# A planner that serves its transfer queue first come, first served: one line of the scheduling rule and a table of offsets

## The chip, the cores and the metric

The kernel runs on one core of a Trainium2 chip. The metric is device time in microseconds for one execution. The five engines are called PE (TensorE), DVE (VectorE), ACT (ScalarE), POOL (GpSimd) and SP (SyncE, which here issues nearly all transfers).

## The reference

Eight batches, eight heads, 576 positions, head size 64. A causal attention with a decay runs first; its output, joined over the heads into a 512-wide row, goes through a small gated block. Cut to what is computed:

```python
scores = 1/sqrt(D) * q @ k.T                          # per batch and head, 576 x 576
cum    = cumsum(log(clip(f, 1e-4, 1)))
scores = where(causal, -1e9, scores + cum[:, None] - cum[None, :])
attn   = exp(scores - max) ; attn /= sum + 1e-9
x      = attn @ v                                     # joined: 8 x 576 x 512
gate   = sigmoid(sum_k conv_w[k] * x shifted by k)    # 5 taps, causal, per channel
out    = (gate * (x @ w_val)) @ w_out
```

All inputs and the output are float32.

## The kernel before, in words

The work is cut into 32 **pairs** (one batch, two heads) and 8 **batches** (four pairs each). For pair i:

- `load_pair`, `load_rest`: transfers bring q, k (`qn`, `kn`, and `zn` for the last 64 rows), v (`vt`) and the decay rows (`dm`, one tile of 128x1280 per head, and `dl` for the last 64 rows). The decay table `decd` is made once at the start and lies in HBM. POOL cuts the causal edge into `dm` (L428) and `dl` (L431).
- `plan_t`: PE transposes q, k (L524) and zn (L531) into a PSUM bank; DVE or ACT copies them out, as one tile for the first four pairs (`Xf`, which lies in the second `gate` tile and is shown under that name) and as a high and a low part afterwards (`Xh`, `Xl`, L515).
- `plan_s`: PE forms the scores (L354, three groups; in the order below `gate1_114` or `Xh`/`Xl`), DVE adds the decay and takes the row extreme (L598), ACT takes the exponential and its sum (L602), DVE takes the reciprocal (L611, L612), and the normalising (`norm`, L374 on ACT, L376 on POOL or DVE) multiplies the rows `P` and `Pl`.
- `plan_pt`: PE transposes `P` (L643) and `Pl` (L661, L662); copies (L369) bring them to `pt`.
- `plan_pv`: PE multiplies `pt` with `vt` (L354, `pt,vt`), the result goes to `x`, is split into `xh` and `xl` (L712), and the five taps of the gate run on DVE (L376, L724).

Per batch, `plan_moe` adds the sigmoid on ACT (L740), the product with `w_val` (`Mv`: L354, `xh`/`xl` with `wall`), the product with the gate (L769), and the product with `w_out` (`Mo`: L354, `wall,hh` and `wall,hl`). The weights arrive in 512 KB pieces in two buffers (`wu` and the tile `ot`) and are decoded by ACT and DVE (L822 to L862).

**What sets the order.** Nothing is emitted in the order of the source. Every step above is a node of `Plan`: a class, the engines that may run it with a cost each, a priority and what it depends on. `Plan.order` then plays the program through: at each turn it looks, for each engine, at the nodes that are ready, takes those that could start within a small slack of the earliest, picks the lowest priority number among them, gives the node to that engine and moves the engine's clock. A node that several engines can run goes where this play puts it first. The result is one fixed list of instructions per engine; on the chip each engine works its list strictly in order, so a node that has to wait holds up all that stands behind it on its engine.

The priority number is the pair's place (`base`) plus an entry of the table `OFF` for the class and the stage of the program. `PEN` is a second table: a penalty on an engine for a class. `STICK` is a bonus on PE for a node of the same tiling as the one before (`mode`).

A transfer is two nodes: `hold`, the issue on SP, and `span`, the transfer itself on an engine of the play that is called `DQ` (L151 to L157). `DQ` stands for the transfer hardware: one server, with the `span` as its cost. Nothing is emitted for it; it only tells the play when the data is there. At most eight transfers are out at a time (L213 to L216).

## Time and profile before

| | us |
|---|---|
| median of 3 runs | 594.59 |
| lowest, highest of these | 593.78, 595.51 |
| the profiled execution's own time | 592.27 |
| its span, first to last instruction | 590.5 |

| engine | busy, us | share of the span |
|---|---|---|
| PE | 558.2 | 95% |
| PE weight load (PEld) | 487.5 | 83% |
| DVE | 461.3 | 78% |
| ACT | 447.9 | 76% |
| POOL | 249.9 | 42% |

Transfers move 93.43 MB in 136294 packets; the mean granted PE clock is 0.977 of full speed. How to read it: the busy shares are means over stages that differ. The profile's slices show a PE clock below 0.9 only within the first fifth of the span, and transfer hardware that is 80% busy or more in five of the first seven slices and in two later ones. So the page is read stage by stage, with the list of who waited for whom beside it.

### The profile page before, as it was taken

What the parts mean: (1) busy time and instruction counts of PE and PEld (TensorE: products, weight loads), DVE (VectorE), ACT (ScalarE), POOL (GpSimd) and SP (SyncE); (2) the same over time, 40 slices, a digit from 0 to 9 for tenths busy, and PEclk for the clock granted to TensorE, in tenths of its full rate; (3) what the DMA queues carried; (4) which work ended last, traced back from release to release, by engine and by line L of the source; (5) the groups of instructions that cost most, each with busy time, mean ns of one, the idle gap of its engine ahead of it and who ended that gap; (6) DMA issues with size and microseconds to landing.
All of it is one profiled execution on the core that took longest, in us unless ns stands there. A gap on an engine that the chain in (4) does not pass through costs nothing.

```text
span 590.5 us, 14025 instructions
## 1 busy us (share of the span) xinstructions
PE 558.2 (95%) x4693; PEld 487.5 (83%) x4693; DVE 461.3 (78%) x1238; ACT 447.9 (76%) x1217; POOL 249.9 (42%) x398
## 2 busy tenths in 40 slices
PE   8778898799889999999999999999999999999997
PEld 7546587689779998889989988899888987889885
DVE  6488979899988797788967897668879789587660
ACT  4688878999878887888887988677798876764511
POOL 3431367334322556456553746455556461210200
PEclk9779699899999999999999999999999999999999
DMA  6979898676465585757866675466776544220012
GB/s 147 266 185 266 170 240 230 166 196 168 114 183 135 143 234 158 188 136 188 188 157 167 184 189 154 117 179 152 193 201 188 159 120 123 80 83 19 37 37 89
DMA packets 136294, 93.43 MB, mean 158 GB/s; under 512 B 118474, under 2 KB 118494, under 8 KB 136222
## 3 DMA queue, kind: packets, MB, share of 16 engines
q1 hardware_dynamic: 136142, 92.52, 59.0%
q8 instruction: 37, 0.61, 0.4%
q14 instruction: 35, 0.29, 0.2%
q10 hardware_dynamic: 80, 0.02, 0.0%
HBM read 82.60 MB, written 9.91 MB: 157 GB/s over the span
## 4 chain that ended last, share of the span: by engine, by line
PE 69%; DVE 13%; DMA 8%; ACT 5%; issue 3%; SPq 1%; POOL 1%; DVEq 0%; POOLq 0%; ACTq 0%
PE banks L354 54%; PE banks L643 9%; DVE banks L598 6%; PE banks L524 3%; DMA wu<-in_moe_w_val_dram 3%; ACT P L602 3%; DMA dm<-decd 2%; DVE gate L724 2%; PE banks L661 2%; DMA qn<-in_q_dram 1%; DVE negm L598 1%; SPq L381 1%; DMA kn<-in_k_dram 1%; PE banks L531 1%; ACT P L374 1%
## 5 line engine op out<-in xcount | busy, mean ns | idle before, releaser
L602 ACT ACTIVATE P<-banks,negm 128x256 f32<-128x256 f32 (+3 forms) x256 | 131.9, 531 | 35.9 <-DVE negm L598 35.6
L369 ACT COPY pt<-banks 128x256 f32<-128x256 f32 (+2 forms) x320 | 116.9, 436 | 42.8 <-PE banks L643 36.4
L598 DVE CUSTOM_DVE_ANT_0 banks<-banks,dm 128x256 f32<-128x256 f32 (+3 forms) x256 | 120.4, 515 | 33.4 <-PE banks L354 22.2
L724 DVE SCALAR_TENSOR_TENSOR gate<-x,cw,gate 128x576 f32<-128x576 f32 x128 | 111.6, 876 | 1.7
L354 PE MATMUL banks<-xh,wall 128*128 128x288 f32 x512 | 110.2, 300 | 1.0 <-ACT ot L369 0.7
L428 POOL TENSOR_SCALAR_AFFINE_SELECT dm<-dm 128x256 f32<-128x256 f32 x126 | 57.5, 481 | 122.0 <-DMA dm<-decd 100.1
L376 POOL TENSOR_SCALAR P<-P,rz 128x128 f32<-128x128 f32 (+3 forms) x132 | 79.0, 614 | 56.5 <-DVE rz L612 32.7
L643 PE MATMUL banks<-ident,P 128*128 128x128 f32 x640 | 93.2, 283 | 9.3 <-POOL P L376 4.1
L354 PE MATMUL banks<-pt,vt 128*64 128x128 f32 (+2 forms) x1408 | 99.0, 294 | 3.2 <-DVE Xl L515 1.9
L354 PEld LDWEIGHTS banks<-pt,vt 128*64 128x64 f32 x1408 | 87.1, 139 | 16.0 <-issue 3.1
L354 PE MATMUL banks<-wall,hh 128*128 128x512 f32 x288 | 92.8, 403 | 2.8 <-ACT P L602 2.6
L643 PEld LDWEIGHTS banks<-ident,P 128*128 128x128 f32 x640 | 74.4, 144 | 20.0 <-POOL P L376 5.3
L354 PEld LDWEIGHTS banks<-xh,wall 128*128 128x128 f32 x512 | 83.8, 188 | 2.8 <-ACT ot L369 1.1
L354 PE MATMUL banks<-xl,wall 128*128 128x288 f32 x256 | 75.4, 294 | 0.0
L712 POOL TENSOR_TENSOR xl<-x,xh 128x576 fp32r<-128x576 f32 x32 | 47.1, 1475 | 46.1 <-ACT xh L369 46.1
L354 PEld LDWEIGHTS banks<-wall,hh 128*128 128x128 f32 x288 | 51.0, 188 | 13.3 <-ACT P L602 3.6
L354 PE MATMUL banks<-Xh 128*128 128x288 f32 (+2 forms) x280 | 59.1, 346 | 1.2 <-DVE Xl L515 1.0
L782 POOL TENSOR_TENSOR hl<-h,hh 128x576 fp32r<-128x576 f32 (+2 forms) x36 | 36.9, 1032 | 48.4 <-ACT hh L369 48.4
L354 PE MATMUL banks<-wall,hl 128*128 128x512 f32 x144 | 56.5, 392 | 0.0
L354 PE MATMUL banks<-Xh,Xl 128*128 128x288 f32 (+2 forms) x280 | 53.6, 315 | 0.0
L354 PE MATMUL banks<-Xl,Xh 128*128 128x288 f32 (+2 forms) x280 | 53.3, 314 | 0.0
L602 ACT ACTIVATION_READ_ACCUMULATOR P<-banks,negm 128x1 f32 x256 | 52.9, 206 | 0.0
(105 smaller groups left out, 916.7 us busy)
## 6 DMA issues: line engine op xcount, KB each, us to landing
dm<-decd SPq DMA_DIRECT2D x62, 640.0 KB, 5.4
out_dram<-ot SPq DMA_DIRECT2D x36, 256.0 KB, 2.1
dl<-decd SPq DMA_DIRECT2D x62, 144.0 KB, 3.8
qn<-in_q_dram SPq DMA_DIRECT2D x64, 128.0 KB, 3.6
kn<-in_k_dram SPq DMA_DIRECT2D x64, 128.0 KB, 5.8
vt<-in_v_dram SPq DMA_DIRECT2D x64, 128.0 KB, 2.9
zn<-in_k_dram SPq DMA_DIRECT2D x32, 32.0 KB, 3.1
vt<-in_v_dram SPq DMA_DIRECT2D x32, 32.0 KB, 3.2
```

The lines of the kernel that those rows point to most:

```text
L354: nc.tensor.matmul(out, lhsT=lhsT, rhs=rhs, start=start, stop=stop)
L369: (eng.copy if eng is nc.scalar else eng.tensor_copy)(out=out, in_=in_)
L376: eng.tensor_scalar(out=out, in0=in_, scalar1=col, scalar2=0.0, op0=ALU.mult, op1=ALU.add)
L428: nc.gpsimd.affine_select(out=t, in_=t, pattern=[[0, 2], [-1, P]], base=0, channel_multiplier=1, compare_op=ALU.is_ge, fill=-BIG)
L524: nc.tensor.transpose(out=bank(key)[:, n * P:(n + 1) * P], in_=src[:, n].rearrange("p h d -> p (h d)"), identity=ident)
L598: nc.vector.tensor_tensor_reduce(out=sl, in0=sl, in1=add[:, o:o + ext], op0=ALU.add, op1=ALU.min, scale=-0.125, scalar=3.0e38, accum_out=n ...
L602: nc.scalar.activation(out=dst[:, o:o + ext], in_=bank(key)[:, c0:c0 + ext], func=AF.Exp, bias=negm[r][:, col], scale=-1.0, accum_out=zs[r ...
L643: nc.tensor.transpose(out=bank(key)[:, c:c + P], in_=Pt[m][:, BOFF[b] + P * j:BOFF[b] + P * j + P], identity=ident)
L661: nc.tensor.transpose(out=bank(key)[:, P * j:P * j + P], in_=Pl[r][:, D + P * j:D + P * j + P], identity=ident)
L712: any_("xl", {"POOL": 1.4, "DVE": 0.67}, p, lambda eng: eng.tensor_tensor(out=xl[s], in0=xv, in1=xh[s][:, :].bitcast(F32), op=ALU.subtract ...
L724: eng.scalar_tensor_tensor(out=gt, in0=src, scalar=wt_, in1=gt, op0=ALU.mult, op1=ALU.add)
L782: eng.tensor_tensor(out=hl[jj][:, y:y + x1 - x0], in0=h32[:, x0:x1], in1=hh[jj][:, y:y + x1 - x0].bitcast(F32), op=ALU.subtract)
```

## The change

One expression of `order` is changed, together with the numbers it was tuned with. For a candidate on `DQ` the rank is no longer the node's priority but `at[n][e]`, the moment from which it could be served, so transfers are played in the order in which they became ready on the queue. `STICK` goes from 18.18 to 18.86, and nearly all entries of `OFF` and `PEN` get new values, most of them within some ten units of the old. No instruction is added or removed apart from how the play divides work: the same nodes, the same costs.

```diff
-STICK = 18.18
+STICK = 18.86
 OFF = {
-    "X": (67.59, 130.9, 49.48, 80.47, -2.55, 2.49),
+    "X": (78.48, 133.4, 48.9, 77.64, -2.11, -4.23),
-    "dec": (1.61, 60.01, -75.88, -13.59, 48.06, 86.54),
+    "dec": (-7.7, 57.47, -85.79, -27.71, 40.96, 74.69),
...
                     pen = PEN.get((nd["cls"], e), NONE)[nd["phase"]] if len(nd["engs"]) > 1 else 0.0
-                    cand.append((t + pen, nd["prio"] - (STICK if e == "PE" and nd["mode"] == mode else 0.0), n, t))
+                    cand.append((t + pen, at[n][e] if e == "DQ" else nd["prio"] - (STICK if e == "PE" and nd["mode"] == mode else 0.0), n, t))
```

Three places of the program show what this moves. In these lists `P0`, `Pl0` and so on are the buffers (with the builder's number behind the underscore), and the shape is the instruction's output.

**Place A**, POOL, pair 0 and the arrival of pair 1's first decay tile. Before:

```order
L376 TENSOR_SCALAR P0_83<-P0_83,rz0_97 128x512
L428 AFFINE_SELECT dm2_70<-dm2_70 128x2x128 x2
L376 TENSOR_SCALAR P0_83<-P0_83,rz0_97 128x256
L376 TENSOR_SCALAR P1_84<-P1_84,rz0_97 128x256
L376 TENSOR_SCALAR P0_83<-P0_83,rz0_97 128x128
L376 TENSOR_SCALAR P1_84<-P1_84,rz0_97 128x384
L376 TENSOR_SCALAR P1_84<-P1_84,rz0_97 128x128
L376 TENSOR_SCALAR Pl0_86<-Pl0_86,rz0_97 128x576
```

The same place now:

```order
L376 TENSOR_SCALAR P0_83<-P0_83,rz0_97 128x512
L376 TENSOR_SCALAR P0_83<-P0_83,rz0_97 128x256
L376 TENSOR_SCALAR P1_84<-P1_84,rz0_97 128x256
L376 TENSOR_SCALAR P0_83<-P0_83,rz0_97 128x384
L428 AFFINE_SELECT dm2_70<-dm2_70 128x2x128 x2
L376 TENSOR_SCALAR P1_84<-P1_84,rz0_97 128x128
L376 TENSOR_SCALAR Pl0_86<-Pl0_86,rz0_97 128x576
```

Three more normalisings now stand ahead of the causal cut of `dm2`, and two behind it; the 128-wide one of `P0` and the 384-wide one of `P1` went to ACT.

**Place B**, PE around the transposes of pair 4 (`qn0`, `kn0`, `zn0`), and SP where their loads are issued. PE before:

```order
L531 MATMUL banks_129<-ident_64,zn1_78 128x128 x2
L643 MATMUL banks_129<-ident_64,P2_85 128x128 x4
L643 MATMUL banks_129<-ident_64,P0_83 128x128 x4
L354 MATMUL banks_129<-gate1_114 128x384 x2
L354 MATMUL banks_129<-gate1_114 128x128 x2
L524 MATMUL banks_129<-ident_64,qn1_74 128x128 x4
L524 MATMUL banks_129<-ident_64,kn1_76 128x128 x4
L661 MATMUL banks_129<-ident_64,Pl1_87 128x128 x4
L662 MATMUL banks_129<-ident_64,Pl1_87 64x128
L524 MATMUL banks_129<-ident_64,qn0_73 128x128 x4
L524 MATMUL banks_129<-ident_64,kn0_75 128x128 x4
L531 MATMUL banks_129<-ident_64,zn0_77 128x128 x2
```

PE now:

```order
L531 MATMUL banks_129<-ident_64,zn1_78 128x128 x2
L524 MATMUL banks_129<-ident_64,qn0_73 128x128 x4
L524 MATMUL banks_129<-ident_64,kn0_75 128x128 x4
L531 MATMUL banks_129<-ident_64,zn0_77 128x128 x2
L643 MATMUL banks_129<-ident_64,P2_85 128x128 x4
L354 MATMUL banks_129<-gate1_114 128x384 x2
L354 MATMUL banks_129<-gate1_114 128x128 x2
L524 MATMUL banks_129<-ident_64,qn1_74 128x128 x4
L524 MATMUL banks_129<-ident_64,kn1_76 128x128 x4
L643 MATMUL banks_129<-ident_64,P0_83 128x128 x4
L643 MATMUL banks_129<-ident_64,P1_84 128x128 x4
L531 MATMUL banks_129<-ident_64,zn1_78 128x128 x2
```

The transposes of pair 4 went from the end of this piece to its start, a transpose of `P1` and one of pair 5's `zn1` were drawn in, and the transposes of `Pl1` with the first `pt,vt` product of pair 1 follow behind. SP before:

```order
L381 DMA zn1_78<-in_k_dram 64x2x64
L381 DMA wu_127<-in_moe_w_val_dram 128x1024
L381 DMA ot_125<-in_moe_w_val_dram 128x1024
L381 DMA qn0_73<-in_q_dram 128x4x64 x2
L381 DMA zn0_77<-in_q_dram 64x64 x2
L381 DMA kn0_75<-in_k_dram 128x4x64 x2
L381 DMA zn0_77<-in_k_dram 64x2x64
```

SP now:

```order
L381 DMA zn1_78<-in_k_dram 64x2x64
L381 DMA qn0_73<-in_q_dram 128x4x64 x2
L381 DMA zn0_77<-in_q_dram 64x64 x2
L381 DMA kn0_75<-in_k_dram 128x4x64 x2
L381 DMA zn0_77<-in_k_dram 64x2x64
L381 DMA wu_127<-in_moe_w_val_dram 128x1024
L381 DMA ot_125<-in_moe_w_val_dram 128x1024
```

The seven issues for pair 4 passed the two weight pieces.

**Place C**, PE after the first batch's sigmoid. Before:

```order
L524 MATMUL banks_129<-ident_64,kn0_75 128x128 x4
L643 MATMUL banks_129<-ident_64,P2_85 128x128 x4
L661 MATMUL banks_129<-ident_64,Pl1_87 128x128 x4
L662 MATMUL banks_129<-ident_64,Pl1_87 64x128
L354 MATMUL banks_129<-Xh1_80 128x288
L354 MATMUL banks_129<-Xh1_80,Xl1_82 128x288
L354 MATMUL banks_129<-Xl1_82,Xh1_80 128x288
```

The same place now:

```order
L524 MATMUL banks_129<-ident_64,kn0_75 128x128 x4
L643 MATMUL banks_129<-ident_64,P2_85 128x128 x4
L661 MATMUL banks_129<-ident_64,Pl1_87 128x128 x4
L662 MATMUL banks_129<-ident_64,Pl1_87 64x128
L354 MATMUL banks_129<-xh0_101,wall_126 128x288
L354 MATMUL banks_129<-xl0_107,wall_126 128x288
L354 MATMUL banks_129<-xh0_101,wall_126 128x288
```

24 `Mv` products of batch 0 now stand between the transposes of `Pl1` and the `pt,vt` products of pair 5; before, six score products and a zn transpose stood there and `Mv` began behind the `pt,vt` products. In the same way the six `Xh0` 128x288 score products of pair 4 now stand ahead of pair 2's `pt,vt` products, and before they stood behind the first half of them.

28 lines of the change are left out of this document (14 added, 14 removed), and 44 rows, old and new, of tables (OFF, PEN).

## The prediction

> **What bounds the kernel now.** The first view is the busy time of each engine in stretches of the program. A row gives the stretch, its length, the busy time of PE, PEld, DVE, ACT and POOL, the granted PE clock, the transfer hardware's busy share and its rate.
>
> ```profile
> 16.00:62.00 46.00, 35.75 (x245) 25.74 (x245) 33.15 (x90) 35.34 (x96) 17.55 (x29) 0.85 0.94 241
> 62.00:120.00 58.00, 49.97 (x428) 42.00 (x428) 51.61 (x143) 50.52 (x144) 27.55 (x49) 0.88 0.78 196
> 120.00:180.00 60.00, 55.79 (x472) 48.80 (x471) 53.50 (x138) 53.60 (x135) 20.75 (x25) 1.00 0.63 172
> 180.00:480.00 300.00, 298.40 (x2690) 269.56 (x2688) 241.10 (x655) 244.94 (x685) 162.33 (x252) 1.00 0.63 167
> 480.00:545.00 65.00, 63.46 (x535) 55.25 (x531) 49.75 (x142) 41.11 (x113) 13.28 (x17) 1.00 0.30 89
> 545.00:590.50 45.50, 41.09 (x261) 35.23 (x260) 21.12 (x40) 13.96 (x27) 3.49 (x2) 1.00 0.14 53
> ```
>
> From 180 to 480 us PE idles 1.6 us in 300: an order of the same work can win nearly nothing there. From 16 to 120 us PE idles 10.25 + 8.03 = 18.3 us, and the clock is at 0.85 and 0.88, so that part of its busy time ran at half speed. This is where the order decides. In the first 46 us the transfers are busy for 94% of the time at 241 GB/s, so there the queue is the resource whose model was changed. The second view is the list of whom PE waited for from 16 to 120 us (total, times, longest):
>
> ```profile
> PE banks L524 <- ACT P L602: 4.0, 3, 2.2
> PE banks L643 <- POOL P L376: 3.4, 1, 3.4
> PE banks L643 <- ACT P L374: 3.3, 3, 2.9
> PE banks L354 <- DVE Xl L515: 1.9, 2, 1.0
> PE banks L531 <- DMA zn<-in_k_dram: 0.9, 1, 0.9
> ```
>
> Few single waits make up the idle time, so the change is worth what it does to each. The timelines of before show them.
>
> **Place A, 16 to 32 us.** Start, length, engine and, in brackets, the idle time before:
>
> ```profile
> 6.08 1.80 SPq L381 DMA_DIRECT2D vt<-in_v_dram  x3
> 21.01 0.77 POOL L428 TENSOR_SCALAR_AFFINE_SELECT dm<-dm 128x256 f32<-128x256 f32 x2 [4.41 <-DMA dm<-decd]
> 21.76 2.20 POOL L376 TENSOR_SCALAR P<-P,rz 128x256 f32<-128x256 f32 x5
> 22.29 2.85 PE L643 MATMUL banks<-ident,P 128*128 128x128 f32 x12 [3.45 <-POOL P L376]
> 24.96 1.12 PE L661 MATMUL banks<-ident,Pl 128*128 128x128 f32 x4
> 23.92 0.98 POOL L376 TENSOR_SCALAR Pl<-Pl,rz 128x576 f32<-128x576 f32 x1
> 25.66 0.68 ACT L822 ACTIVATE gate<-ot 128x512 f32<-128x512 uint32 x1
> 31.72 0.69 DVE L598 CUSTOM_DVE_ANT_0 banks<-banks,dm 128x512 f32<-128x512 f32 x1
> ```
>
> POOL stood 4.41 us in front of the cut of `dm2`, with five normalisings behind it that need nothing from it, and PE stood 3.45 us behind those. The change puts three more normalisings first, so this wait goes. But it isn't worth 3.45 us, because `P1` 128 and `Pl0` still stand behind `dm2`, and PE has to pass them before pair 0's `pt,vt` product. `dm2` itself comes later: SP has two more issues ahead of the decay table's store (0.6 us each, 1.80 for three), so 0.7 to 1.1 us, landing near 21.9. From there POOL needs 0.77 + 0.44 (a fifth of 2.20) + 0.98 = 2.2 us, so `Pl0` is ready at 24.1 against 24.9. Next late is DVE, which decodes a weight piece until it can begin pair 1 at 31.72; it gains up to 1 us at L822, and loses about half of that since ACT's next step in it (L830) now stands behind the first copy of `x`. Bounds: 0 and -0.8; I take **-0.5 us**.
>
> **Place B, 44 to 62 us.** PE and ACT, and a row of the chain of waits:
>
> ```profile
> 46.68 0.33 PE L531 MATMUL banks<-ident,zn 128*128 128x128 f32 x1 [0.91 <-DMA zn<-in_k_dram]
> 46.84 1.04 PE L643 MATMUL banks<-ident,P 128*128 128x128 f32 x8
> 47.81 1.14 PE L354 MATMUL banks<-gate 64*128 64x384 f32 x8
> 50.22 0.66 PE L661 MATMUL banks<-ident,Pl 128*128 128x128 f32 x4 [0.25 <-ACT pt L369]
> 53.18 1.53 PE L354 MATMUL banks<-pt,vt 128*64 128x128 f32 x24
> 47.84 0.68 ACT L822 ACTIVATE gate<-wu 128x512 f32<-128x512 uint32 x1 [1.48 <-DMA wu<-in_moe_w_val_dram]
> 39.33 8.42 DMA wu<-in_moe_w_val_dram
> ```
>
> Before, `zn1` landed at 46.6 and `wu`, issued behind it, at 47.75. Now pair 4's loads stand between: four of 128x4x64 and three small ones, 590 KB. At the stretch's 241 GB/s that is 2.4 us; at the rate at which `wu` followed `zn1` (524 KB in 1.1 us) it is 1.3 us. So PE, which now comes to pair 4's transposes directly behind `zn1`, stands there until 47.9 to 49.0, and with its small work in between comes to `P2` 1.5 to 2.5 us later than 46.84. From there the piece up to the `pt,vt` product, with four transposes at 0.66, is 0.7 (`P2`) + 1.1 (scores) + 1.3 (`qn1`, `kn1`) + 1.3 (`P0`, `P1`) + 0.4 (pair 5's `zn1`) + 1.0 (`Pl1`) = 5.8 us, which gives 54.1 to 55.1 against 53.18. Of this some 1.1 us (`P1`, `zn1`) is work brought forward: -0.2 to +0.8. Pair 5's `zn1` stands behind two weight pieces on the queue, 1049 KB or 2.2 to 4.4 us at the same two rates, and PE may wait up to 1 us for it. On the other side ACT's 1.48 us before `wu` go, since the exponentials now stand ahead of L822, and the high and low parts of pair 4 are made earlier. Queued behind PE's new wait are pair 2's transposes, which ACT's copies and pair 1's product await. Bounds: -0.2 and +1.8; I take the middle, rounded up, **+0.9 us**.
>
> **62 to 76 us.** The PE timeline:
>
> ```profile
> 64.56 0.79 PE L524 MATMUL banks<-ident,kn 128*128 128x128 f32 x4 [1.45 <-ACT P L602]
> 65.28 2.47 PE L354 MATMUL banks<-gate 64*128 64x384 f32 x8
> 67.68 1.12 PE L643 MATMUL banks<-ident,P 128*128 128x128 f32 x4
> 71.51 2.83 PE L354 MATMUL banks<-pt,vt 128*64 128x128 f32 x24 [0.71 <-ACT P L602]
> ```
>
> The transpose of `kn1` waited 1.45 us for a bank that pair 3's exponential had to leave; it now stands ahead of pair 3's scores and can't wait for those. The bank is then short for the next `P` transposes instead, so I count half of it: -0.7 (bounds 0 and -1.45). The 0.71 us before the product of pair 2 are filled by pair 4's six score products: -0.7 (bounds 0 and -0.7). Together **-1.4 us**. The same rows show the half clock: eight 64x384 products took 2.47 us here and 1.14 at 47.81, 24 `pt,vt` products 2.83 here and 1.53 at 53.18.
>
> **Place C, 105 to 118 us.**
>
> ```profile
> 108.47 0.66 PE L524 MATMUL banks<-ident,kn 128*128 128x128 f32 x4 [2.19 <-ACT P L602]
> 114.00 3.06 PE L354 MATMUL banks<-pt,vt 128*64 128x128 f32 x44 [0.86 <-DVE Xl L515]
> 117.32 0.40 PE L354 MATMUL banks<-xh,wall 128*128 128x288 f32 x1 [0.26 <-ACT x L369]
> ```
>
> The wait of 2.19 us behind the sigmoid stays: the same transposes stand there. The 0.86 and 0.26 us are covered by the 24 `Mv` products that now stand ahead; DVE's order has the decode of the last piece of `w_val` ahead of them. Bounds: 0 (the wait comes back once `Mv` has been used up) and -1.1; I take **-0.9 us**.
>
> **The rest.** PE changes its tiling 163 times instead of 160, counted in the two orders. What that costs:
>
> ```profile
> 80.87 0.27 PE L354 MATMUL banks<-Xh,Xl 64*128 64x128 f32 x2
> 80.98 0.27 PE L354 MATMUL banks<-Xl,Xh 64*128 64x128 f32 x2
> 81.19 0.66 PE L524 MATMUL banks<-ident,qn 128*128 128x128 f32 x4
> ```
>
> Without a change the next row starts 0.11 us later, with one 0.21: three times 0.1 is **+0.3 us**. From 120 to 545 us the many moved rows are hidden by a PE that has next to no idle time; if the cover went, it could only cost. From the last batch's first `Mv` product to the end PE's order is the same row for row: 0.
>
> The sum is -0.5 + 0.9 - 1.4 - 0.9 + 0.3 = -1.6 us. The profiled execution took 592.27 us (590.5 of span and 1.8 around it), so 590.7 us of its own time. The median of the runs shown is 2.3 us above it; the change goes onto that, 594.59 - 1.6 = **593.0 us**. From 0.3% on, 1.8 us, a measurement of this kernel can tell a change from none.
>
> **The rivals.**
>
> *The clock holds.* If the waits of 62 to 76 us shrink far enough, PE keeps full speed there. By the rows above that saves 2.47 - 1.14, 1.12 - 0.66 and 2.83 - 1.53 us, and as much as the second of these again for the transposes of `Pl`: 3.5 us. With the other half of the 1.45 us and place B made good (-0.9) the sum is -1.6 - 3.5 - 0.7 - 0.9 = -6.7, 587.9 us. For it: pair 4 is further on, and ACT no longer stands before `wu`. Against it: place B puts a new wait ahead of that stretch. At place A the long wait is followed by slow work:
>
> ```profile
> 89.10 1.51 PE L643 MATMUL banks<-ident,P 128*128 128x128 f32 x12 [0.30 <-DVE Xl L515]
> ```
>
> against 2.85 us for the same twelve at 22.29. [...]
>
> *Slower: place B turns cold.* PE's wait for pair 4's loads falls into a stretch that is already thin. If the clock drops there, the 5.7 us behind it run at up to half speed, and by the prices just worked out some 3.5 us are lost. With the +1.8 of the upper bound instead of +0.9, and nothing won at 62 to 76 us (+1.4), the sum is -1.6 + 0.9 + 1.4 + 3.5 = +4.2, 598.8 us; with those two it ends 0.7 us above the time before without any lost speed, and slower by over 0.3% from 1.1 us of it on. For it: in-order PE, loads at 94% busy. Against it: ACT and DVE gain slack there.
>
> *The rule does next to nothing.* The order of the issues on SP still goes by priority, and from 120 us on PE is full; the shifts would cancel within 0.3%: 594.6 us.
>
> **How the numbers follow.** The forecast, with a range of its own from 591.5 to 594.5 us, has 0.42; of it 0.16 lie below 592.8 (faster by over 0.3%) and 0.26 above. The clock that holds has 0.27, place B turning cold 0.23, no effect 0.08. So faster is 0.16 + 0.27 = 0.43, the same 0.26 + 0.08 = 0.34, slower 0.23. The range has to reach into both outer cases: down to 586.0 (the rival's 587.9 with some of place A's clock) and up to 598.5.
>
> **What would show it.** In the changed profile: POOL's wait before `dm2` has four normalisings ahead of it and PE's 3.45 us are gone, with a shorter wait before `Pl0`. PE waits 1 to 2 us for `qn`/`kn` loads just after pair 3's `zn`. No wait of 0.7 us stands before pair 2's `pt,vt` product and none of 0.86 before pair 5's. The stretch from 180 us on is as long as before within 1 us. The prediction is wrong if PE's idle time up to 120 us changes by more than 3 us either way, if the clock of the two stretches leaves 0.82 to 0.91, or if the time comes from behind 180 us.

## The result

| | before | changed |
|---|---|---|
| median, us (6 runs each, side by side) | 594.19 | 599.12 |
| lowest, highest | 593.72, 596.95 | 597.27, 605.04 |
| the profiled execution's own time | 592.27 | 605.04 |
| its span, first to last instruction | 590.5 | 603.3 |
| mean granted PE clock | 0.977 | 0.969 |

The change makes the kernel slower by 1.2% (ratio 1.0122, interval 1.0083 to 1.0161). The prediction was 593.0 us with a range up to 598.5: the direction was wrong, and the time lies just outside. The two profiled executions lie at the fast end of the one kernel's times and at the slow end of the other's, so their difference of 12.8 us overstates the 5 us between the medians. One execution of the kernel before, at 600.70 us, counts as a slow one and is left out of all that follows.

The stretches of the prediction, in the changed kernel's profile (stretch, length, busy time of PE, PEld, DVE, ACT and POOL, PE clock, transfer share, GB/s):

```profile
16.00:62.00 46.00, 33.23 (x224) 24.68 (x223) 29.64 (x83) 31.37 (x88) 11.16 (x22) 0.81 0.82 220
62.00:120.00 58.00, 47.86 (x396) 39.33 (x393) 52.91 (x142) 49.26 (x140) 34.25 (x54) 0.88 0.79 204
120.00:180.00 60.00, 57.26 (x453) 49.45 (x452) 50.57 (x126) 51.67 (x125) 17.82 (x21) 0.94 0.48 136
180.00:480.00 300.00, 293.57 (x2629) 262.86 (x2628) 239.81 (x639) 244.40 (x681) 158.34 (x242) 1.00 0.64 169
480.00:545.00 65.00, 63.93 (x555) 56.23 (x554) 51.83 (x152) 45.61 (x128) 21.23 (x30) 1.00 0.41 120
545.00:603.30 58.30, 54.09 (x376) 47.53 (x374) 31.14 (x65) 20.02 (x44) 3.73 (x2) 1.00 0.12 46
```

From 16 to 120 us PE now idles 12.8 + 10.1 = 22.9 us against 18.3, and from 180 to 480 us 6.4 against 1.6. The second number was not expected at all. Of the prediction's own signs of being wrong, this profile shows all three: PE's idle time up to 120 us is 4.7 us longer (more than 3), the clock of the first stretch is 0.81 (below 0.82), and time comes from behind 180 us. The list of whom PE waited for from 16 to 120 us (total, times, longest; its first three entries) has a new kind of entry, a single wait of 3.3 us for DVE:

```profile
PE banks L643 <- POOL P L376: 4.7, 3, 2.7
PE banks L354 <- ACT P L602: 3.8, 2, 2.1
PE banks L524 <- DVE Xl L515: 3.3, 1, 3.3
```

**Place B** is where that wait stands. SP, ACT, DVE and PE in the timeline, with the idle time before in brackets:

```profile
44.07 1.13 SPq L381 DMA_DIRECT2D zn<-in_q_dram  x2
47.28 0.59 SPq L381 DMA_DIRECT2D wu<-in_moe_w_val_dram  x1
53.56 0.67 ACT L822 ACTIVATE gate<-wu 128x512 f32<-128x512 uint32 x1 [3.92 <-DMA wu<-in_moe_w_val_dram]
53.56 0.43 DVE L824 TENSOR_SCALAR gate<-wu 128x512 int32<-128x512 int32 x1 [3.77 <-DMA wu<-in_moe_w_val_dram]
54.65 1.12 PE L524 MATMUL banks<-ident,qn 128*128 128x128 f32 x4 [3.27 <-DVE Xl L515]
59.26 2.94 PE L354 MATMUL banks<-pt,vt 128*64 128x128 f32 x44
```

The weight piece `wu` was issued at 47.28 us, behind pair 4's loads; before, at 39.33. ACT and DVE reach its decode and stand almost 4 us. The copy (`Xl`) that empties the bank of pair 4's first transposes stands behind that decode on DVE, so PE stands 3.27 us before its next transposes, and the product of pair 1 begins at 59.26, not at the 54.1 to 55.1 us that were predicted. This reads like the prediction's rival "place B turns cold", whose 598.8 us is also nearly the time measured. The experiments do not bear it out.

### The profile page after: what moved, and what is told of

The parts are those of the page before. It is cut to its first block, busy times and chain, and to the rows that moved or that the text cites. A ratio compares the mean times of both kernels' runs of the same rounds, so it can differ in the third digit from the quotient of the medians.

```text
span 603.3 us, 14030 instructions
## 1 busy us (share of the span) xinstructions
PE 563.7 (93%) x4693; PEld 490.9 (81%) x4693; DVE 466.1 (77%) x1236; ACT 450.6 (75%) x1222; POOL 253.5 (42%) x395
## 3 DMA queue, kind: packets, MB, share of 16 engines
q1 hardware_dynamic: 136142, 92.52, 57.3%
## 4 chain that ended last, share of the span: by engine, by line
PE 62%; DVE 13%; ACT 10%; DMA 9%; issue 3%; POOL 1%; SPq 0%; DVEq 0%; POOLq 0%; ACTq 0%
PE banks L354 48%; PE banks L643 7%; DVE banks L598 6%; ACT P L602 5%; PE banks L524 3%; DVE gate L724 2%; DMA dm<-decd 2%; DMA dl<-decd 2%; PE banks L661 2%; DMA kn<-in_k_dram 2%; ACT pt L369 1%; DMA wu<-in_moe_w_out_dram 1%; DVE Xh L369 1%; DVE negm L598 1%; DMA wu<-in_moe_w_val_dram 1%
## 5 line engine op out<-in xcount | busy, mean ns | idle before, releaser
L602 ACT ACTIVATE P<-banks,negm 128x128 f32<-128x128 f32 (+3 forms) x256 | 132.1, 529 | 43.2 <-DVE negm L598 42.8
L598 DVE CUSTOM_DVE_ANT_0 banks<-banks,dm 128x128 f32<-128x128 f32 (+3 forms) x256 | 120.6, 516 | 30.2 <-PE banks L354 18.8
L724 DVE SCALAR_TENSOR_TENSOR gate<-x,cw,gate 128x576 f32<-128x576 f32 x128 | 114.1, 893 | 1.9
L354 PEld LDWEIGHTS banks<-pt,vt 128*64 128x64 f32 x1408 | 87.5, 140 | 13.7 <-issue 3.6
L643 PEld LDWEIGHTS banks<-ident,P 128*128 128x128 f32 x640 | 72.9, 142 | 25.2 <-POOL P L376 8.1
L712 POOL TENSOR_TENSOR xl<-x,xh 128x576 fp32r<-128x576 f32 x32 | 48.9, 1529 | 52.4 <-ACT xh L369 52.4
L354 PE MATMUL banks<-Xh 128*128 128x288 f32 (+4 forms) x280 | 59.7, 347 | 2.8 <-ACT pt L369 1.3
L354 PEld LDWEIGHTS banks<-wall,hh 128*128 128x128 f32 x288 | 50.8, 188 | 13.7 <-DVE Xl L515 2.9
L354 PE MATMUL banks<-Xh,Xl 128*128 128x288 f32 (+4 forms) x280 | 54.3, 317 | 0.0
L354 PE MATMUL banks<-Xl,Xh 128*128 128x288 f32 (+4 forms) x280 | 53.9, 317 | 0.0
```

Source lines behind the costliest of these rows:

```text
L354: nc.tensor.matmul(out, lhsT=lhsT, rhs=rhs, start=start, stop=stop)
L598: nc.vector.tensor_tensor_reduce(out=sl, in0=sl, in1=add[:, o:o + ext], op0=ALU.add, op1=ALU.min, scale=-0.125, scalar=3.0e38, accum_out=n ...
L602: nc.scalar.activation(out=dst[:, o:o + ext], in_=bank(key)[:, c0:c0 + ext], func=AF.Exp, bias=negm[r][:, col], scale=-1.0, accum_out=zs[r ...
L643: nc.tensor.transpose(out=bank(key)[:, c:c + P], in_=Pt[m][:, BOFF[b] + P * j:BOFF[b] + P * j + P], identity=ident)
L712: any_("xl", {"POOL": 1.4, "DVE": 0.67}, p, lambda eng: eng.tensor_tensor(out=xl[s], in0=xv, in1=xh[s][:, :].bitcast(F32), op=ALU.subtract ...
L724: eng.scalar_tensor_tensor(out=gt, in0=src, scalar=wt_, in1=gt, op0=ALU.mult, op1=ALU.add)
```

## The experiments

Each run stands beside runs of the kernel before on the same chip. In the edits, `force` is the list of each engine's nodes as the changed kernel's play makes them; `move(engine, nodes, node)` puts nodes ahead of another one in that list, and the program is emitted by the edited list with the same PSUM banks. A node is named by its class (`T` the transposes of q, k and zn, `TH`/`TL` their copies, `wvD` the load and `wv` the decode of a `w_val` piece, `PE` the copies out of a bank, `conv` a tap), its base and its place among equals. The letters of the theories are explained where they are first used.

One way of reading is used throughout. An execution's span times its mean granted clock is my estimate of what it would take at full clock with the same idle time; I call it the **work and idle** part, and the rest of the span the **lost** part. In the profiles the first is 545.5 us plus PE's idle time on average, between 543.5 and 548.1 for every kernel here but the rule alone (542.0). So it follows the idle time to within some 2 us in one profile. Since each execution has its span and its clock on record, the two parts can be told apart without a profile.

| run | median, us | ratio (interval) | work and idle, lost (medians) | PE idle in its profile: 0 to 120, 120 to 480, 480 to end |
|---|---|---|---|---|
| before, first profile | 594.19 | | 580.2, 13.7 (110 executions: five chips and e5) | 20.5, 5.8, 6.0 |
| changed, first profile | 599.12 | 1.0122 (1.0083, 1.0161) | 584.7, 13.7 | 25.2, 9.2, 5.3 |
| e1 changed again | 599.96 | 1.0068 (1.0040, 1.0095) | 583.3, 14.3 | 24.1, 9.1, 5.0 |
| e5 before again | 595.42 | 1.0011 (0.9983, 1.0039) | 581.0, 14.0 | 21.0, 6.9, 6.3 |
| e3 rule only | 629.10 | 1.0553 (1.0521, 1.0585) | 599.1, 27.3 | 24.3, 25.8, 8.5 |
| e4 tables only | 595.88 | 0.9994 (0.9965, 1.0023) | 583.2, 9.2 | 23.1, 9.0, 5.0 |
| e6 old, then new from pair 1's product | 606.86 | 1.0200 (1.0164, 1.0236) | 586.1, 18.8 | 27.5, 8.6, 5.1 |
| e7 new, then old from pair 1's product | 602.88 | 1.0134 (1.0095, 1.0174) | 587.0, 14.7 | 24.5, 9.3, 9.5 |
| e8 tables, rule from pair 1's product | 601.83 | 1.0118 (1.0081, 1.0154) | 587.7, 13.2 | 25.5, 10.5, 5.9 |
| e2 `wu` first | 601.43 | 1.0090 (1.0059, 1.0121) | 585.4, 15.6 | 25.1, 9.0, 5.9 |
| e9 decode late | 601.92 | 1.0132 (1.0081, 1.0184) | 584.6, 14.0 | 23.5, 10.1, 5.1 |
| e10 place B undone | 602.61 | 1.0155 (1.0109, 1.0202) | 585.8, 15.0 | 25.8, 8.3, 5.3 |
| e11 tap behind | 596.67 | 1.0037 (1.0003, 1.0071) | 582.5, 11.9 | 22.4, 8.3, 5.0 |
| e12 e10 and e11 | 600.52 | 1.0112 (1.0072, 1.0152) | 584.2, 14.1 | 28.4, 8.5, 5.3 |
| e13 pair 5's zn late | 605.09 | 1.0159 (1.0111, 1.0207) | 586.5, 16.9 | 27.9, 9.4, 5.5 |
| e14 e10 and e13 | 607.71 | 1.0216 (1.0168, 1.0263) | 587.5, 20.4 | 29.1, 9.1, 5.4 |
| e15 changed, half decay tiles | 599.13 | 1.0067 (1.0036, 1.0098) | 584.2, 13.4 | 21.2, 10.8, 5.0 |
| e16 before, half decay tiles | 594.44 | 0.9977 (0.9944, 1.0010) | 580.4, 12.4 | 22.4, 7.2, 6.3 |
| e17 old, then new from pair 4's product | 599.04 | 1.0062 (1.0034, 1.0090) | 582.0, 15.5 | 23.1, 9.2, 5.0 |
| e18 new, then old from pair 4's product | 601.15 | 1.0075 (1.0040, 1.0109) | 583.3, 14.7 | 24.2, 5.2, 9.0 |

### This execution, the rule, or the tables

The theories here: A, the weights come late at place B; B, the slow profile is a chance of the clock; C, the loss is smeared over the whole order. Run e1 is the changed kernel as it is, profiled again.

> The changed kernel itself once more, for a second profile: which of its lost microseconds come in every execution. Theory A (weights late): pair 4's loads now pass the weight piece wu on SP, wu lands at 53.5 instead of 47.75 us, ACT and DVE stand 3.9 and 3.8 us in front of it and PE 3.3 us behind them; this comes back in every profile, with PE 3 to 4 us late by 62 us, and the time is 598 to 600. Theory B (clock by chance): the loss is made of half-speed windows that fall differently from run to run; the second profile shows other windows (the one at 153 to 160 us gone) and PE is less than 2 us late by 62 us. Theory C (smeared): most of the loss comes behind 180 us, in small waits, in this profile too (3 us or more).

Place B in its profile:

```profile
42.03 1.20 SPq L381 DMA_DIRECT2D zn<-in_q_dram  x2
45.26 0.59 SPq L381 DMA_DIRECT2D wu<-in_moe_w_val_dram  x1
49.16 0.69 ACT L822 ACTIVATE gate<-wu 128x512 f32<-128x512 uint32 x1 [0.41 <-DMA wu<-in_moe_w_val_dram]
50.24 0.66 PE L524 MATMUL banks<-ident,qn 128*128 128x128 f32 x4 [0.20 <-DVE Xl L515]
53.21 0.52 PE L531 MATMUL banks<-ident,zn 128*128 128x128 f32 x2 [1.00 <-ACT P L602]
54.85 2.95 PE L354 MATMUL banks<-pt,vt 128*64 128x128 f32 x44
```

The same program issues `wu` 2 us earlier, ACT waits 0.41 us for it and not 3.92, and PE 0.20 and not 3.27. The product begins at 54.85 us, as predicted. So what the first profile shows at place B comes in some executions and not in others, and A, by which it comes in every one, falls. This execution took 597.83 us, 2.2 above the median before on its chip (595.62), and its work and idle part is 584.2 us, no shorter than the 584.6 of the first profile. How many of the other executions behind the median of 599.96 had the late piece isn't known, since they have no profile.

Runs e3 and e4 take the change apart. The edit of e3 against the kernel before:

```diff
-                    cand.append((t + pen, nd["prio"] - (STICK if e == "PE" and nd["mode"] == mode else 0.0), n, t))
+                    cand.append((t + pen, at[n][e] if e == "DQ" else nd["prio"] - (STICK if e == "PE" and nd["mode"] == mode else 0.0), n, t))
```

> The one line of the rule alone, with the tables of before. On SP wu and ot stay in front of pair 4's loads, but from there on many rows move. Theory A (weights late, which the new tables do and not the rule): no wait of ACT or DVE over 2 us for wu at 45 to 55 us, time within 2 us of 594. Rival (the rule itself makes worse orders): 597 or more, without the wu wait.

The rule alone costs 5.5%. Its profile has a window row, entries of PE's list of waits, and a step of the chain that tell where:

```profile
120.00:240.00 120.00, 100.64 (x774) 88.38 (x775) 78.70 (x196) 83.02 (x215) 32.41 (x42) 0.89 0.40 111
```

```profile
PE banks L354 <- DVE h L769: 6.7, 1, 6.7
PE banks L354 <- DVE Xl L515: 5.9, 2, 5.4
```

```profile
125.21 7.74 DMA ot<-in_moe_w_out_dram
```

From 120 to 240 us PE idles 19.4 us. A piece of `w_out` lands at 132.9, and DVE stands 1.23 us for it. DVE works the decodes of several weight pieces one after the other, and batch 0's product with the gate (L769), which has to leave the bank that PE needs, stands behind them. With the old offsets the new rule gathers the weights' decode ahead of work that PE waits for; what in the play makes it do so is not shown.

Run e4 has the changed tables and keeps the old rule:

```diff
-                    cand.append((t + pen, at[n][e] if e == "DQ" else nd["prio"] - (STICK if e == "PE" and nd["mode"] == mode else 0.0), n, t))
+                    cand.append((t + pen, nd["prio"] - (STICK if e == "PE" and nd["mode"] == mode else 0.0), n, t))
```

> The new tables with the old rule. The order is the changed kernel's but for some hundred PE rows between about 45 and 95 us and their loads; wu still stands behind pair 4's loads on SP. Theory A (weights late): the 3.8 us waits for wu are there, time 597.5 to 600. Rival (the rule itself costs): the time goes back to 594 to 595.

The tables alone make no difference: 0.9994, interval 0.9965 to 1.0023. On PE the order differs from the changed kernel's in some hundred rows, all between about 53 and 83 us of e1's profile; behind them PE's list is the same to the end. But its parts are not those of before: work and idle is 3 us longer, as in the changed kernel, and the lost part 4.5 us shorter.

This is the closest pair of the series. On one chip the one line of the rule, with the new tables in both, takes the median from 595.88 to 599.96 us; the intervals of the two ratios (0.9965 to 1.0023, and 1.0040 to 1.0095) do not meet. So the new tables make up for most of what the rule spoils. In the means, the tables bring 3.6 us of work and idle and take away 3.5 us of lost time, and the rule brings 4.1 us of lost time back, with work and idle the same to within 0.6. What in those hundred rows costs the clock is not shown.

Run e5 is the kernel before, profiled a second time.

> The kernel before once more, for a second profile: its first one, 592.27 us, is as low as the lowest of 23 later times (592.29 to 599.45, median 595.62), so a row of the changed kernel may look late beside it that is not. Theory D (early stretch): this profile comes out near 595.6, up to 3 us later than the first, and it loses that behind 120 us, as the changed kernel's second profile does (even with before's at 137 us, 4 to 6 us behind it from 204 us on); then the changed kernel's own loss is what it has up to pair 2's product. Theory E (later order): this profile is still ahead of the changed kernel's second one by 4 us or more at 240 us though both were even at 137 us.

It gives 1.0011, and PE idles 34.2 us in it against 32.3 in the first. That is the yardstick for the idle times of single profiles: a difference of 2 us between two of them is nothing.

### Which half of the order

D puts the loss into the early stretch, E into the later order. Runs e6 and e7 play both orders and join them; e8 has the new tables and changes the rule at the seam. The expectations place the seam at pair 2's first `pt,vt` product, some 71 us in. The edit places it at pair 1's: a product node's `base` is its pair's number plus 0.6, so the first one at or above 1.5 is that of pair 1, which stands at 53.18 us in the kernel before and at 54.85 in e1. The three runs therefore divide the order at about 53 to 60 us.

```diff
+    first, second = played(plan, True), played(plan, False)      # old, new; e7 the other way round
+    cut = next(i for i, (e, n) in enumerate(first) if plan.nodes[n]["cls"] == "PV" and plan.nodes[n]["base"] >= 2 - 0.5)
+    done = set(n for e, n in first[:cut])
+    merged = first[:cut] + [(e, n) for e, n in second if n not in done]
```

> The order of before up to pair 2's first pt,vt product (about 71 us), with places A and B in it, and from there on the work that is left in the changed kernel's order; banks are handed out anew. Theory D (early stretch): as fast as before, 594.5 to 596.5. Theory E (the later order costs 4 us): 599 to 601.

> The reverse: the changed kernel's order up to pair 2's first pt,vt product, and the order of before from there on. Theory D (early stretch): as slow as the changed kernel, 599 to 601. Theory E (the later order): 594.5 to 596.5. If both this and the reverse come out at 597 to 598, the loss lies on both sides.

> The new tables throughout; up to pair 2's first pt,vt product the old rule sets the order, behind it the new rule's. Against the changed kernel that moves 19 rows of PE and 34 of SP (zn and kn of pair 3 and one qn go behind the decay loads dm and dl) and some of ACT and DVE. The old rule throughout gave 595.9, the new rule 600.0. Theory D (early stretch): 595 to 597. Theory E (later order): 599 to 601.

None of the three is faster than the changed kernel (1.0122 and 1.0068): 1.0200, 1.0134 and 1.0118. A joined order has waits of its own at the seam. In e6 PE stands there for a load that the first order had no reason to bring early:

```profile
60.16 0.66 PE L531 MATMUL banks<-ident,zn 128*128 128x128 f32 x2 [5.46 <-DMA zn<-in_q_dram]
```

So these three decide nothing between D and E.

### Place B taken away, in several ways

Run e2 issues the two weight pieces ahead of pair 4's seven loads, as before the change; e9 moves the decode on DVE and ACT to where `wu` has landed; e10 undoes place B on SP, PE and DVE.

```diff
+    wv = [n for n in sp if plan.nodes[n]["cls"] == "wvD"][1:3]
+    at = sp.index(wv[0]) - 7
+    sp[:] = [n for n in sp if n not in wv]
+    sp[at:at] = wv
```

> The changed kernel's lists of PE, ACT, DVE and POOL and its banks as they are; only on SP the two weight pieces wu and ot go back in front of pair 4's seven loads (qn, zn, kn), where they were before. Theory A (weights late): the 3.9, 3.8 and 3.3 us waits of ACT, DVE and PE for wu go, minus up to 1 us that pair 4's transposes wait longer for their loads: 595 to 596.5. Theory B or C (clock by chance, or smeared): the waits move to the loads and the time stays at 598 to 600.

```diff
+    move("DVE", [("wv", 1.7, 0), ("wv", 1.7, 1), ("wv", 1.7, 2)], ("wv", 1.7, 3))
+    move("ACT", [("wv", 1.7, 0), ("wv", 1.7, 1)], ("PE", 1.5))
```

> The changed kernel with its loads and PE's list as they are. Only the first steps of the decode of the weight piece wu (ACT's L822 and L830, DVE's L824, L826, L828) go behind pair 2's four reductions on DVE and four exponentials on ACT, so a late wu holds up nothing else. The changed kernel's two profiles differ by 5.5 us by 125 us: where wu came late (53.5 us) PE stood 3.3 us and the work behind ran at half clock; where it came at 50 us it didn't. Theory F (two causes: place B turns cold in about half of the executions, and waits behind 137 us cost some 3 us in all of them): the slow half goes, median 597 to 598.5, and no execution much above 600. Rival (what PE waits for there is the queue, whatever stands in front): the wait moves to the loads or to wu's later steps, median 599 to 601.

```diff
+    move("SP", [("wvD", 1.2), ("wvD", 1.9)], ("load", 3.0, 0))
+    move("PE", [("T", 4.0), ("T", 4.02), ("T", 4.04)], ("PV", 1.6))
+    move("DVE", [("TH", 4.0), ("TL", 4.0)], ("TH", 4.02))
```

> The changed kernel with place B as it was before on all engines: on SP wu and ot in front of pair 4's loads; on PE pair 4's transposes behind pair 1's Pl instead of right behind zn; on DVE the two copies of its first transposes behind wu's decode. The earlier run that moved the loads alone only exchanged the wait for wu (3.3 us) against one for qn (3.1 us). Theory F: with the transposes out of the way PE waits less than 1 us there and the median is 596.5 to 598.5. Rival (place B is chance, the loss is all elsewhere): 599 to 600.5.

None is clearly faster than the changed kernel (1.0122 and 1.0068): 1.0090, 1.0132, 1.0155. With `wu` first, PE stands for pair 4's `qn` instead:

```profile
50.29 1.08 PE L524 MATMUL banks<-ident,qn 128*128 128x128 f32 x4 [3.14 <-DMA qn<-in_q_dram]
```

and with place B undone for pair 5's `zn` and for a later `qn`, which the rest of the new order asks for as early as before:

```profile
53.03 0.45 PE L531 MATMUL banks<-ident,zn 128*128 128x128 f32 x2 [3.86 <-DMA zn<-in_q_dram]
65.47 0.66 PE L524 MATMUL banks<-ident,qn 128*128 128x128 f32 x4 [1.84 <-DMA qn<-in_q_dram]
```

The next theory, F, was that place B is cold in half of the executions and that fixed waits behind 137 us do the rest. Run e13 moves pair 5's zn transpose back, e14 does that with e10; e11 puts a tap of the gate on DVE behind the decay of the next scores and a copy of `pt` on ACT ahead of a weight's decode, for PE's waits near 148 us, and e12 does that with e10.

```diff
+    move("PE", [("T", 5.04)], ("T", 5.02))
```

> The changed kernel with one move on PE: the transpose of pair 5's zn goes from in front of pair 1's Pl (53 to 58 us) to in front of pair 5's kn (about 65 us); before, it stood at 68.6 us. Theory G (the queue is the bound up to 62 us, and the new PE order asks it for pair 4's loads and pair 5's zn some 10 to 15 us earlier than before; whichever wait is taken away, PE stands at the next load): wu is still in front, so most of the loss stays; the waits of 1 to 2 us for zn go, 597.5 to 599.5. Rival (the early loss has nothing to do with what is asked of the queue): 599 to 602.

> Place B as before on all engines (weights first, pair 4's transposes behind pair 1's Pl) and pair 5's zn late as well. With place B alone undone PE stood 3.9 us at pair 5's zn, and the time was 602.6. Theory G: that wait goes and nothing else stands on a load up to 60 us, so 596 to 598.5, and 4 us or more below the run without this move. Rival: 600 to 603.

```profile
68.17 1.09 PE L524 MATMUL banks<-ident,kn 128*128 128x128 f32 x4 [5.78 <-DMA kn<-in_k_dram]
```

This row of e13 shows what comes instead: PE stands 5.78 us for a `kn`. The loads share one queue (q1 moves 92.52 of the 93.43 MB in the page of before), and in these edits a wait taken out in one place let PE run up to the next load. Both are much slower (1.0159, 1.0216).

```diff
+    move("DVE", [("conv", 5.98)], ("TH", 9.04))
+    move("ACT", [("PE", 7.44)], ("wo", 5.7, 1))
```

> The changed kernel with one move on DVE and one on ACT near 145 us: the gate's tap that took 2.06 us goes behind the four reductions of pair 8's scores, and one copy to pt ahead of a decode step and of the cast of hh. In every profile of the new orders PE waits 0.8, 0.7 and 0.2 us there and then runs at half clock until about 153 us (24 products of pt,vt in 2.2 to 2.8 us instead of 1.5). Theory F: those 1.7 us and the cold stretch (1.8 us and more) go, median 596.5 to 598. Rival (a wait taken away there comes back before the next sigmoid): 599 to 600.5.

> Both of the last two together: place B as before, and the tap behind the reductions. Theory F: the gains add up, 593.5 to 596, level with the kernel before or faster. Rival: at least one of the two is given back, 597 or more.

Run e11 has the lowest median of the edits, 596.67 (1.0037, interval 1.0003 to 1.0071). But its reason does not hold, for PE still stands at 148 us in its profile:

```profile
145.12 0.50 PE L354 MATMUL banks<-Xh 64*128 64x512 f32 x2 [0.65 <-ACT x L369]
149.18 0.44 PE L354 MATMUL banks<-Xh 64*128 64x384 f32 x1 [1.25 <-ACT P L602]
```

and together with e10 nothing is left of the gain. What made e11 better isn't known.

### The queue's load taken away

G puts the loss on the queue's early demand: the new order asks for more, earlier. Two decay tiles, the second of pair 2 and the first of pair 3, are fetched at half width, in the changed kernel (e15) and in the kernel before (e16). The other half of each tile is left as it was, so the rows of these two heads come out as other numbers.

```diff
-            load("dec", 1.6, p + 0.05 * h, dm[m], decd[2 * i + h:2 * i + h + 1, 0:SW].to_broadcast([P, SW]), dk, [("dm", m)])
+            load("dec", 1.6, p + 0.05 * h, dm[m][:, 0:SW // (1 + (2 * i + h in (5, 6)))], decd[2 * i + h:2 * i + h + 1, 0:SW // (1 + (2 * i + h in (5, 6)))].to_broadcast([P, SW // (1 + (2 * i + h in (5, 6)))]), dk, [("dm", m)])
```

> Measures the queue by itself: the changed kernel with the two decay tiles that are issued together at 35.5 us (pair 2's second head, pair 3's first) loaded to half their width only; the other half keeps what an earlier pair left in it, so the rows of these two heads come out as other numbers. 655 KB less stand on the queue, 2.7 us at the 241 GB/s of this stretch. Theory G: the second of the two lands at 42 instead of 44 us, SP goes on 2 us earlier, PE's wait behind wu falls below 1 us, the stretch behind keeps its clock: 595.5 to 597.5. Rival (the loss is in the order of the computing engines): 599 or more.

> The same two half-width decay tiles in the kernel before (the same two heads come out as other numbers). Theory G: before asks less of the queue there (its waits for loads were 0.9 us on PE, 1.5 on ACT), so it gains at most 1 us: 593.5 to 595.5, and the two kernels come within 2.5 us of each other, against 4 to 5 us with whole tiles. Rival: both gain alike, and the distance stays at 4 to 5 us.

In the profile of e15 PE's longest wait for a load up to 62 us is under 0.9 us, and its idle time up to 120 us is down to 21.2. And yet the two kernels stay 599.13 - 594.44 = 4.7 us apart, with 3.8 us of it in work and idle. G falls as far as these two tiles go: with whole tiles the distance is 4.3 to 4.9 us.

### Joined later

K puts the loss behind 115 us, L ahead of it. The orders are joined again, later. By the numbering told above the seam lies at pair 4's first `pt,vt` product (95.14 us in the kernel before) and not at pair 5's, which the expectations name. On PE this makes no difference, as both orders run alike from there to place C, some 111 us in; DVE and POOL pass to the second order at about 100 us.

```diff
-    cut = next(i for i, (e, n) in enumerate(first) if plan.nodes[n]["cls"] == "PV" and plan.nodes[n]["base"] >= 2 - 0.5)
+    cut = next(i for i, (e, n) in enumerate(first) if plan.nodes[n]["cls"] == "PV" and plan.nodes[n]["base"] >= 5 - 0.5)
```

> The order of before up to pair 5's first pt,vt product (about 114 us) and the rest in the changed kernel's order; banks handed out anew. The seam lies behind the fullest stretch of the queue this time. Theory K (the steady loss lies behind 115 us: the profiles of all kernels with the new order are 2 to 4 us later at 150 us and 4 to 5 us later at 320 us than both profiles of before, although the good ones are level with them at 137 us; what happens at place B only scatters the executions): 598 to 600. Theory L (it lies ahead of 115 us): 594.5 to 596.5. A wait of more than 1 us at 105 to 125 us that neither kernel has would be the seam's own and is taken off.

> The reverse: the changed kernel's order up to pair 5's first pt,vt product, the order of before from there on. Theory K: 594.5 to 596.5, and PE's idle time behind 120 us like that of before (11.8 and 13.2 us in its two profiles, against 14.1 and 14.5). Theory L: 598.5 to 600.5.

Either half alone costs 0.6 to 0.75%, against 0.7 and 1.2% for the whole. Read by the idle times, e17 has the later order's 9.2 us from 120 to 480, e18 the old one's 5.2. But neither is clean: the profile of e17 idles 23.1 us up to 120, where PE's order is the old one but for the last 9 us, and e18 has at its end a wait that neither kernel has:

```profile
513.25 1.15 PE L643 MATMUL banks<-ident,P 128*128 128x128 f32 x8 [2.21 <-ACT x L369]
```

Its end idles 2.7 to 3.0 us more than that of the kernel before. Less this, an estimate from the two rows of the table, some 0.4 to 0.9 us of work and idle are left for the early half (583.3 - 580.2 - 2.7 and the same against 579.7, the median of its own chip), and 1.8 to 2.3 for the later one. That leans to K without settling it.

## Why the prediction was wrong

**What the loss is made of.** Over the executions of the unedited kernels the work and idle part is 580.2 us on average before (110 executions, standard deviation 1.9) and 583.7 changed (16, standard deviation 1.6): 3.5 us more. The lost part is 13.4 and 14.0: no clear difference, with standard deviations of 2.7 and 2.9. So against the kernel before most of the loss reads as idle time of PE. This is a balance and not yet a cause: e4 has the same work and idle part as the changed kernel and is as fast as the kernel before, because it loses less to the clock. Where the idle time lies is read from the windows. Before, first profile:

```profile
0.00:62.00 62.00, 49.53 (x320) 36.65 (x321) 44.27 (x126) 43.78 (x117) 22.50 (x54) 0.89 0.86 216
62.00:80.00 18.00, 15.42 (x103) 12.43 (x104) 13.84 (x38) 14.12 (x42) 6.66 (x14) 0.72 0.80 194
80.00:120.00 40.00, 34.55 (x329) 29.57 (x326) 37.77 (x105) 36.40 (x103) 20.89 (x36) 0.96 0.78 197
120.00:480.00 360.00, 354.19 (x3159) 318.36 (x3157) 294.60 (x791) 298.54 (x820) 183.08 (x277) 1.00 0.63 168
480.00:590.50 110.50, 104.54 (x795) 90.49 (x790) 70.87 (x181) 55.08 (x139) 16.77 (x19) 1.00 0.23 74
```

The changed kernel, second profile (e1), the one without the late `wu`:

```profile
0.00:62.00 62.00, 47.56 (x316) 35.16 (x317) 42.92 (x126) 43.54 (x117) 21.74 (x52) 0.89 0.83 212
62.00:80.00 18.00, 15.13 (x135) 11.29 (x137) 16.49 (x45) 15.71 (x44) 10.98 (x16) 1.00 0.89 237
80.00:120.00 40.00, 33.24 (x306) 28.98 (x301) 37.19 (x99) 34.56 (x97) 23.05 (x38) 0.91 0.70 186
120.00:480.00 360.00, 350.94 (x3088) 312.41 (x3088) 291.87 (x768) 297.18 (x811) 179.63 (x268) 1.00 0.63 167
480.00:596.10 116.10, 111.09 (x863) 97.46 (x859) 78.25 (x203) 60.18 (x157) 21.00 (x24) 1.00 0.23 74
```

The row from 120 to 480 us in the other two profiles, first e5 and then the changed kernel's first:

```profile
120.00:480.00 360.00, 353.12 (x3141) 317.09 (x3141) 293.82 (x789) 297.15 (x814) 182.21 (x277) 1.00 0.62 167
120.00:480.00 360.00, 350.82 (x3080) 312.30 (x3079) 290.38 (x764) 296.07 (x805) 176.16 (x263) 0.99 0.61 163
```

Length less PE's busy time, as the mean of both profiles of each kernel, against the prediction's terms:

| stretch | predicted | idle before | idle changed | found |
|---|---|---|---|---|
| 0 to 62 (places A and B) | -0.5 + 0.9 | 12.4 | 14.7 | +2.3 |
| 62 to 80 | -1.4 | 2.5 | 3.1 | +0.6 |
| 80 to 120 (place C) | -0.9 | 5.8 | 6.8 | +1.0 |
| 120 to 480 | 0 | 6.3 | 9.1 | +2.8 |
| 480 to the end | 0 | 6.1 | 5.1 | -1.0 |

The sum is 5.7, some 2 us more than in the mean over all executions. Both profiles of the kernel before lie on the low side of its scatter (576.9 and 578.4 us of work and idle, against 580.2). Which rows have these 2 us too many can't be told from two profiles. The row from 120 to 480 us is the firmest: in all 14 profiles that have the new order there with the new tables, PE idles 8.3 us or more, and in four of the five with the old order 7.2 or less (the fifth is e7 with 9.3, whose seam lies some 60 us earlier).

**Place A (-0.5): the wait moved and did not shrink.** PE and its idle times in the changed kernel's first profile:

```profile
23.47 0.33 PE L643 MATMUL banks<-ident,P 128*128 128x128 f32 x1 [2.68 <-POOL P L376]
24.19 1.12 PE L661 MATMUL banks<-ident,Pl 128*128 128x128 f32 x4 [0.39 <-POOL Pl L376]
25.45 2.72 PE L354 MATMUL banks<-pt,vt 128*64 128x128 f32 x28
```

The three normalisings went ahead as described, but `P1`'s last piece behind `dm2` takes their place as the one PE stands for: 2.68 + 0.39 us here and 3.55 + 0.25 in e1, against 3.45 and, in the second profile of before, about 3.0. The prediction had this order of events and sized the gain small; none can be told from the scatter, since the `pt,vt` product begins at 25.45 and 25.88 us now and began at 26.22 and 25.52. The gain from "some of place A's clock", which the lower end of the range (586.0 us) counts in, is shown by no run. Eleven of the twelve transposes that stood at 22.29 us before now stand ahead of the wait and run at full clock (1.00 from 16.7 to 20.8 us), but the half clock stands behind the wait as before: 0.50 from 24.2 to 25.4 us, with 1.12 us for the transposes of `Pl` as before and as in e1, and 0.097 us for each of the 28 products against 0.064 of the 24 that the prediction quotes at 53.18.

**Place B (+0.9; up to 1.8): the size about right in e1, by another way, and far too small in the first profile.** The forecast wait of PE for pair 4's `qn` and `kn` hardly came: none in e1, 0.51 us in the first profile. The transposes of `P2` begin at 48.37 us in e1, the early end of the forecast (48.3 to 49.3), and what comes behind them are waits that were not forecast, 0.20 us for the copies on DVE, 1.00 for a bank that ACT's exponential has to leave, and 0.43 for a copy. In e1 the product begins within the forecast times all the same; that is luck, not the mechanism. What was left out is SP. The seven loads put ahead of `wu` delay it also by the time that SP stands before one of them, while the prediction counted the queue's rate only. SP goes on at 42.03 us in e1 and at 44.07 in the first profile, there after 2.6 us of waiting for a decay tile to land; from its issue the weight piece then takes 3.9 us to land in e1 and 6.3 in the first profile. Both together make the 4.4 us by which it is later: in the one case the decode just meets its piece, in the other DVE and ACT stand nearly 4 us. The step said that ACT's 1.48 us "go": they shrink to 0.41 in one execution and grow to 3.92 in another.

**62 to 76 us (-1.4): the two waits went, others came.** The transpose of `kn` waits 0.57 us and not 1.45, and in the first profile no wait stands before pair 2's product (in e1 one of 0.84 us stands one row ahead of it). But the same profile has, on PE:

```profile
68.72 0.66 PE L643 MATMUL banks<-ident,P 128*128 128x128 f32 x4 [0.68 <-ACT pt L369]
71.47 2.74 PE L354 MATMUL banks<-gate 64*128 64x384 f32 x8 [2.09 <-ACT P L602]
110.52 0.33 PE L643 MATMUL banks<-ident,P 128*128 128x128 f32 x1 [1.37 <-POOL P L376]
114.48 1.12 PE L524 MATMUL banks<-ident,kn 128*128 128x128 f32 x4 [2.05 <-ACT P L602]
```

The scores that fill the gap ahead of the product now wait themselves, for the bank and for the copies of `pt` on ACT: 0.68 and 2.09 us (1.10 in e1). The prediction allowed for this by halving one of the waits; the whole gain was lost, and by the table 0.6 us more.

**Place C (-0.9).** The 0.86 and 0.26 us are gone in both profiles, and the 2.05 us behind the sigmoid stay, as predicted. The third row above is what came instead: 1.37 us for a normalising on POOL (1.80 in e1).

**"From 120 to 545 us the many moved rows are hidden: 0".** This step failed, and it was argued from a row that could not carry it. A PE that idles 1.6 us in 300 says that little can be won there; it does not say that another order keeps it so full. And the prediction's own row for 120 to 180 us shows 4.2 us of idle time in 60. Hundreds of rows are moved in that stretch; from 180 to 480 us PE idles 6.4 and 5.5 us in the two profiles of the changed kernel, against 1.6 and 2.6. The longest waits come in both of them. PE in the first:

```profile
151.74 0.66 PE L643 MATMUL banks<-ident,P 128*128 128x128 f32 x4 [0.84 <-ACT pt L369]
153.07 0.44 PE L354 MATMUL banks<-Xh 64*128 64x384 f32 x1 [0.68 <-ACT P L602]
157.43 2.83 PE L354 MATMUL banks<-pt,vt 128*64 128x128 f32 x24
182.23 0.40 PE L354 MATMUL banks<-xh,wall 128*128 128x288 f32 x1 [1.39 <-DVE Xl L515]
312.63 0.73 PE L354 MATMUL banks<-wall,hh 128*128 128x512 f32 x2 [0.98 <-DVE Xl L515]
363.83 0.44 PE L643 MATMUL banks<-ident,P 128*128 128x128 f32 x2 [1.43 <-POOL P L376]
```

The prediction had no rival that lay behind 120 us. The same sentence added "if the cover went, it could only cost", and put nothing into the range for it.

**Which step failed.** Two did. The gains of places A and C and of 62 to 80 us, -2.8 us together, were counted as the waits that would go, with little for those that would come in their place: in both pairs of profiles PE's idle time up to 120 us rose, by 3.9 us in the mean, where the terms of places A, B, C and of 62 to 80 us add up to -1.9. And the 0 behind 120 us was +1.8 (2.8 up to 480 us, less 1.0 at the end). By these windows the early gains are the larger error; by the joined orders the two are about equal (an estimate of 0.4 to 0.9 us where -1.9 was forecast, and of 1.8 to 2.3 where 0 was). The sum left the clock as it was, and against the kernel before this came true on balance, but out of two changes that cancel (e4) and that the prediction did not have.

**The rivals.** "Slower: place B turns cold" gave 598.8 us and the sign. A cold stretch is seen in the first profile, where the clock from 54.65 to 57.5 us, behind PE's 3.27, is 0.50, but e1 has as long a work and idle part without it, three ways of removing it gained nothing, and over 16 executions the lost part is that of before. That its number was nearly met is luck. A clock lost elsewhere between 53 and 83 us is not excluded: against e4 the whole difference is lost time. "The clock holds" happened in a piece of e1 (the clock from 62 to 80 us is 1.00 and not 0.72) and was given back elsewhere (0.91 and not 0.96 from 80 to 120). "The rule does next to nothing" is refuted by e3 and e4: with the old tables it costs 5.5%, with the new ones 4 us.

**What stays open.** How the 3.5 us divide between the stretch up to 120 us and the one behind it, since the joined orders bring waits of their own. Why e11 is nearer to the kernel before than any other edit. Why the tables alone run at a better clock (0.984, median of 12) than the changed kernel (0.976, median of 10 in e1); in the means this is all that the rule costs with the new tables. No version is faster than the kernel before: the tables alone equal it, and e16 leaves part of the work out.

## What to carry to other kernels

A nearly full engine bounds what a new order can win, not what it can lose: where an order is made anew from end to end, the stretches without slack need a cost of their own in the range. On engines that work in order, a wait that is removed is worth what the next one behind it leaves over; here, with the loads on one queue, the next one was the following load in e2, e10 and e13 (3.14, 3.86 and 5.78 us). Before a wait seen in one profile is made the reason, profile the same program again, and compare span times clock over all executions: that separates idle time from clock where a single profile can't. A balance of the two against one kernel is not a cause: take the parts of the change one by one, as in e3 and e4, and look at both again.

## What the runs showed of the hardware

The mean granted clock of one program is not the same from one execution to the next: 0.968 to 0.988 for the kernel before, with times from 590.8 to 599.6 us, the longer ones at the lower clock. At a span of 595 us 0.01 of clock is 6 us in the lost part if nothing else moves; a line through the 110 executions gives 3.3 us for it.

PE was at half clock behind several short waits as well as behind a long one. Behind the 3.45 us of place A in the kernel before, the clock from 22.3 to 25.1 us is 0.50. In the changed kernel's first profile the waits at 151 to 154 us are 0.84, 0.68 and 0.23 us, the clock from 154 to 157 us is 0.50, and the 24 products at 157.43 take 2.83 us against 1.53 at 53.18 us in the kernel before, where the clock is 1.00; in e1 the same place has 2.23. None of these three waits is a third of place A's, so in this place the half clock came without one unbroken wait of that length.

The same load of the same program let SP go on at 42.03 us in one execution and at 44.07 in another, and the 512 KB weight piece that SP issued 3.2 us later took 3.9 and 6.3 us to land. The two together decided whether DVE and ACT stood nearly 4 us for it.
